# Interleaving scores with smaller v pieces, pairing head pairs in the weighted values, and beginning the first dense layer on half of its input

## The chip, the cores and the metric

One core of a Trainium2 chip runs the whole program. The metric is the device time of one execution, in microseconds. Where I speak of "the control", I mean the kernel before, run again beside each experiment on the same chip. The experiments ran on three chips, so each is held against its own control.

The engines are PE (TensorE, matmuls; PEld is its weight loads), DVE (VectorE), ACT (ScalarE) and POOL (GpSimd). PSUM is where the matmuls of this kernel put their results. The profile names tiles: tq is q transposed, ks the sorted k, tv the sorted v in PSUM and vs its copy ("eviction"), sc the scores and at their exponentials, pv the weighted values, rec their reciprocals and x the product, tr the transposed x and xt its copy, hps the first layer in PSUM, rt its rectifier output, wp the result of a filler.

## The reference, cut to what matters

```python
# P: sort_net after 5 rounds of exp and of row and column normalisation
k_sorted = einsum('bhij,bhjcd->bhicd', P, k_blocks)     # same for v
scores   = q_b @ k_sorted.T / 8
attn     = softmax(scores)                              # within blocks of 96
x        = (attn @ v_sorted), heads side by side        # 3072 x 512
h        = x @ w_in                                     # 512 -> 2048
out      = (s * relu(h)**2 + b) @ w_out                 # 2048 -> 512
```

There are 4 batches of 8 heads, 768 rows and 64 columns a head, in 8 blocks of 96 rows. The kernel works on half batches of 384 rows. Two heads make a head pair; four head pairs make the 512 inputs of the first layer. The whole argument is about the first half batch, that is, about how soon after its start PE can be given the dense layers.

## The kernel before

The pieces that matter, with cuts marked. `psa` is a pool of three PSUM buffers of 1024 floats a partition (the large pool), `psb` of two buffers of 512 (the small pool). "v" and "s" name the engine that copies a result out of PSUM, DVE or ACT. `n0` and `nn` choose blocks: the first layer takes two of the half batch's four blocks at a time.

```python
def warm_up(n, pool=psb):                  # filler: keeps PE occupied, result unused
    wp = pool.tile([128, 256], FP, ...)
    for _ in range(n):
        nc.tensor.matmul(out=wp, lhsT=zt[:, 0:128], rhs=zt, start=True, stop=True)

def v_piece0(d0, n, eng):                  # sort v of batch 0, n of its 64 columns
    ps = psa.tile(...) if n > 8 else psb.tile(...)
    for t in range(n):                     # 64 rows in use
        nc.tensor.matmul(out=ps[:, t, :], lhsT=vb[0:64, :, d0 + t], rhs=pd1[0:64]..., ...)
    evac(VS[0][:, :, d0:d0 + n], ps..., eng)

def s_piece(t, hp): ...                    # 8 score matmuls into psa, one exp on ACT -> AT[t, hp]
def p_piece(t, hp, n0, nn): ...            # weighted values of one head pair; DVE: reciprocal, product -> X
def t_part(t, hp0, eng, n0, nn): ...       # transpose two head pairs of X into XT

def ffn1(t, slot, n0, nn):                 # first layer
    for f0 in range(0, NF, 2):
        hps = psa.tile(...)                # 2 x 4 matmuls over the four head pairs
        ... relu on ACT, square on DVE ...
        slot()                             # one piece of other work

warm_up(76); build_pd1(); q_half(0, "s")
k_piece(0, 0, 16, 1, "v")(); ... k_piece(0, 80, 8, 1, "s")()
v_piece0(0, 16, "v"); v_piece0(16, 16, "s"); v_piece0(32, 16, "v"); s_piece(0, 0)
v_piece0(48, 8, "v"); s_piece(0, 1)
v_piece0(56, 8, "v"); s_piece(0, 2); s_piece(0, 3)
for hp in range(NHP):
    p_piece(0, hp, 0, 2)
    if hp == 3: t_part(0, 0, "s", 0, 2)
    warm_up(2, psa)
t_part(0, 2, "v", 0, 2)
warm_up(2, psa)
ffn1(0, Queue([P(0,0,2,2), P(0,1,2,2), P(0,2,2,2), P(0,3,2,2), ...], 8), 0, 2)
```

The softmax here doesn't subtract the row's maximum and nothing guards it: scores larger than these inputs give would overflow.

## Time and profile before

| what | value |
|---|---|
| time, first runs | 233.06 us (233.01 to 233.14, 3 runs) |
| span of the profiled run | 231.6 us, PE busy 97% |
| clock of TensorE, by the trace's clock records, which begin at 3.87 us | half from 14.11 to 27.77 us, full otherwise |
| fillers at the start | one each 0.213 us up to 3.9 us, each 0.109 us after |
| first weighted value (pv) | 23.71 us |
| first matmul of the first layer (hps) | 27.32 us by the timeline, 27.52 in the chain |

PE is the bound nearly everywhere. The chain of waits gives, for each piece of the path that ended last, its start, its length and what it was. The timeline gives each engine's instructions and, in brackets, how long the engine had been idle before and what ended that. The lines that carry the reading stand in the prediction below.

A "window" below is a stretch of 3.413 us. That is read off the clock records: in the trace of before the clock rose at 3.87 us, fell at 14.11, rose at 27.77 and fell, past the end, at 232.57, which is 10.24, 13.65 and 204.80 us apart, or 3, 4 and 60 times 3.413.

### The profile page before, as it was taken

What the parts mean: (1) busy time and instruction counts of PE and PEld (TensorE: products, weight loads), DVE (VectorE), ACT (ScalarE), POOL (GpSimd) and SP (SyncE); (2) the same over time, 40 slices, a digit from 0 to 9 for tenths busy, and PEclk for the clock granted to TensorE, in tenths of its full rate; (3) what the DMA queues carried; (4) which work ended last, traced back from release to release, by engine and by line L of the source; (5) the groups of instructions that cost most, each with busy time, mean ns of one, the idle gap of its engine ahead of it and who ended that gap; (6) DMA issues with size and microseconds to landing.
All of it is one profiled execution on the core that took longest, in us unless ns stands there. A gap on an engine that the chain in (4) does not pass through costs nothing.

```text
span 231.6 us, 4837 instructions
## 1 busy us (share of the span) xinstructions
PE 224.3 (97%) x2036; PEld 136.8 (59%) x2036; DVE 116.8 (50%) x245; ACT 114.6 (49%) x164; POOL 48.3 (21%) x62
## 2 busy tenths in 40 slices
PE   8879999999999999999999999999999999999994
PEld 6779887765544555566555555665555556554442
DVE  5778566638992645244446653343452634432221
ACT  6168479685158486856630645656222236660000
POOL 7820000399992000007920000000000000000000
PEclk9975699999999999999999999999999999999999
DMA  5999999998799992764999995610115240001212
GB/s 93 142 200 211 226 193 205 231 220 183 106 110 180 273 312 63 161 82 65 130 148 133 183 197 115 93 47 0 46 47 113 93 110 4 3 0 45 80 59 91
DMA packets 46695, 28.90 MB, mean 125 GB/s; under 512 B 35921, under 2 KB 41041, under 8 KB 46161
## 3 DMA queue, kind: packets, MB, share of 16 engines
q0 software_dynamic: 18800, 15.21, 47.8%
q1 hardware_dynamic: 27728, 13.32, 26.6%
q8 instruction: 16, 0.26, 0.5%
q10 hardware_dynamic: 144, 0.07, 0.1%
q14 instruction: 7, 0.05, 0.1%
HBM read 29.63 MB, written 8.65 MB: 165 GB/s over the span
## 4 chain that ended last, share of the span: by engine, by line
PE 82%; DVE 7%; DMA 5%; ACT 3%; issue 1%; POOL 0%; POOLq 0%
PE hps L473 35%; PE ops L516 31%; DMA qr<-in_q_dram 5%; PE pv L402 4%; PE sc L375 3%; DVE gt L478 2%; ACT ks L240 2%; DVE ks L238 2%; PE tv L320 2%; PE ops L501 2%; PE tk L294 1%; PE tv L350 1%; PE wp L182 1%; PE tq L254 1%; PE tv L336 1%
## 5 line engine op out<-in xcount | busy, mean ns | idle before, releaser
L473 PE MATMUL hps<-xt,wi 128*128 128x384 bf16 (+1 forms) x576 | 87.1, 309 | 0.3 <-ACT rt L477 0.3
L516 PE MATMUL ops<-wo,gt 128*128 128x512 bf16 x368 | 86.9, 380 | 0.4 <-DVE ot L490 0.4
L473 PEld LDWEIGHTS <-wi 128*128 128x128 bf16 x576 | 54.1, 98 | 30.6 <-issue 1.3
L477 ACT ACTIVATE rt<-hps 128x768 bf16<-128x768 f32 (+1 forms) x72 | 53.1, 741 | 37.4 <-PE hps L473 37.0
L478 DVE TENSOR_TENSOR gt<-rt 128x768 bf16<-128x768 bf16 (+1 forms) x72 | 41.2, 574 | 50.2 <-ACT rt L477 50.0
L516 PEld LDWEIGHTS <-gt 128*128 128x128 bf16 x368 | 33.6, 98 | 37.2 <-issue 1.0
L378 ACT ACTIVATE at<-sc 96x768 bf16<-96x768 f32 x32 | 24.4, 804 | 27.7 <-PE sc L375 27.7
L490 DVE SCALAR_TENSOR_TENSOR ot<-ops,s_bc,bias 128x512 f32<-128x512 f32 x23 | 17.1, 749 | 41.2 <-PE ops L516 41.2
L240 ACT CAST ks<-tk 64x512 bf16<-64x512 f32 (+1 forms) x32 | 18.6, 582 | 10.5 <-PE tk L294 10.2
L407 DVE TENSOR_TENSOR x<-pv,rec 96x512 bf16<-96x512 f32 (+1 forms) x36 | 22.6, 627 | 1.3
L639 POOL TENSOR_TENSOR csum<-csum,wo 128x512 f32<-128x512 f32 x14 | 17.6, 1254 | 1.0
L402 PEld LDWEIGHTS <-at 96*128 96x128 bf16 (+1 forms) x256 | 12.0, 104 | 3.8
L182 PE MATMUL wp<-zt 128*128 128x256 bf16 x86 | 12.9, 311 | 1.1 <-DVE warm L113 1.1
L238 DVE CAST ks<-tk 64x512 bf16<-64x512 f32 (+1 forms) x20 | 13.0, 651 | 1.1 <-PE tk L294 0.8
L402 PE MATMUL pv<-vs,at 96*128 96x66 bf16 (+1 forms) x256 | 13.0, 199 | 0.1
L240 ACT CAST vn<-tv 128x512 bf16<-128x512 f32 (+1 forms) x12 | 9.4, 799 | 7.2 <-PE tv L350 5.0
L375 PEld LDWEIGHTS <-ks 64*96 64x96 bf16 x256 | 8.6, 128 | 5.8 <-issue 5.1
L406 DVE RECIPROCAL rec<-pv 96x8 f32<-96x8 f32 (+1 forms) x36 | 6.9, 192 | 9.5 <-PE pv L402 9.4
L84 POOL DMA_DIRECT2D qr<-in_q_dram x12 | 10.6, 912 | 4.8 <-DMA kb<-in_k_dram 3.1
L375 PE MATMUL sc<-qt,ks 64*96 64x96 bf16 x256 | 10.9, 219 | 0.1
L182 PEld LDWEIGHTS <-zt 128*128 128x128 bf16 x86 | 9.0, 110 | 2.6 <-DVE warm L113 1.1
L294 PEld LDWEIGHTS <-kb 64*128 64x128 bf16 x192 | 6.7, 99 | 3.9 <-issue 3.4
(73 smaller groups left out, 98.4 us busy)
## 6 DMA issues: line engine op xcount, KB each, us to landing
out_dram<-ot SPq DMA_DIRECT2D x23, 256.0 KB, 2.4
kb<-in_k_dram POOLq DMA_DIRECT2D x4, 768.0 KB, 12.2
vb<-in_v_dram POOLq DMA_DIRECT2D x4, 768.0 KB, 19.0
wi<-in_moe_w_in_dram POOLq DMA_DIRECT2D x2, 1024.0 KB, 19.7
wo<-in_moe_w_out_dram POOLq DMA_DIRECT2D x2, 1024.0 KB, 32.6
qr<-in_q_dram POOLq DMA_DIRECT2D x12, 128.0 KB, 13.5
dv<-vn SPq DMA_DIRECT2D x6, 256.0 KB, 7.5
vs<-dv POOLq DMA_DIRECT2D x4, 384.0 KB, 12.7
```

Source lines behind the costliest of these rows:

```text
L182: nc.tensor.matmul(out=wp, lhsT=zt[:, 0:128], rhs=zt, start=True, stop=True)
L238: nc.vector.tensor_copy(out=out, in_=in_)
L240: nc.scalar.copy(out=out, in_=in_)
L375: nc.tensor.matmul(out=sc[:, e, n * BLK:(n + 1) * BLK], lhsT=ks[pr, g0 + n, :], rhs=QT[b][pr, hp, q0:q0 + BLK], start=True, stop=True)
L378: nc.scalar.activation(out=at, in_=sc[:, :, 0:TG], func=AF.Exp, scale=scale)
L402: nc.tensor.matmul(out=pv[e][0:m, (n - n0) * VW:(n - n0 + 1) * VW], lhsT=atf[:, c0:c0 + m], rhs=VS[b][:, gi, :], start=True, stop=True)
L407: nc.vector.tensor_tensor(out=x[:, n0:n0 + nn, hp * 128:(hp + 1) * 128].rearrange("p n (e d) -> p e n d", e=2), in0=pvv[:, :, :, 0:D], in1 ...
L473: nc.tensor.matmul(out=hps[:, f, 0:nt], lhsT=wi_at(hp, f0 + f), rhs=xt_at(t, hp, n0, nn), start=(hp == 0), stop=(hp == NHP - 1))
L477: nc.scalar.activation(out=rt[:, :, 0:nt], in_=hps[:, :, 0:nt], func=AF.Relu)
L478: nc.vector.tensor_tensor(out=gt[:, f0:f0 + 2, c0:c0 + nt], in0=rt[:, :, 0:nt], in1=rt[:, :, 0:nt], op=ALU.mult)
L516: nc.tensor.matmul(out=ops, lhsT=gt[:, f, m * 128:(m + 1) * 128], rhs=wo_at(f), start=(f == 0), stop=(f == NF - 1))
L639: nc.gpsimd.tensor_tensor(out=csum, in0=csum, in1=wo_at(f), op=ALU.add)
```

## The change

The intent is to have scores and exponentials ready earlier, to save DVE instructions and fillers between scores and first layer, and to fill the time of the last copy of x with matmuls that don't need it. The core of the diff, with cuts marked:

```diff
+    def p_pair(t, hp0, n0):            # weighted values of two head pairs in one psa tile
+        p2 = psa.tile([128, 4, 256], FP, tag="a", name="pv")
+        ... 16 -> 8 matmuls a pair, ONE reciprocal (96x8) and ONE product (96x512) ...
-    def ffn1(t, slot=nothing, n0=0, nn=HB):
+    def ffn1(t, slot=nothing, n0=0, nn=HB, lead=0):
+        for f0 in range(0, lead, 2):   # first two head pairs only
+            begun[f0] = psa.tile([128, 2, 512], FP, tag="a", name="hps")
+            products(f0, begun[f0], range(0, NHP // 2))
 ...
-    v_piece0(32, 16, "v")
-    s_piece(0, 0)
-    v_piece0(48, 8, "v")
-    s_piece(0, 1)
-    v_piece0(56, 8, "v")
-    s_piece(0, 2)
-    s_piece(0, 3)
     for hp in range(NHP):
-        p_piece(0, hp, 0, 2)
-        if hp == 3:
-            t_part(0, 0, "s", 0, 2)
-        warm_up(2, psa)
+        v_piece0(32 + 8 * hp, 8, "v")
+        s_piece(0, hp)
+    warm_up(2)
+    p_pair(0, 0, 0)
+    warm_up(2)
+    p_pair(0, 2, 0)
+    t_part(0, 0, "s", 0, 2)
+    warm_up(3)
     t_part(0, 2, "v", 0, 2)
-    warm_up(2, psa)
 ...
-    ffn1(0, Queue([...], 8), 0, 2)
+    ffn1(0, Queue([...], 8), 0, 2, 4)
```

## The prediction

Notes on the hardware that came from outside this case are cut from the prediction, with the cuts marked. Its sum: the first weighted value at 24.2, 3.0 of work on PE and 0.05 more give the first layer at 27.25 us; 16 of its matmuls then end at 28.98 in place of 29.17, a gain of 0.19 us, so 233.06 - 0.19 = 232.87 us. In "three runs within 0.13 us speak against that", "that" is the thought that the clock rises at another time in each execution. The 4096 slots of rival A can be had from the trace: sixteen fillers of 256 columns, 0.213 us each, fill a window. That the clock looks at such slots was my guess; part 5 holds it against the traces.

> **What bounds the kernel now.** I read the page's engine table first, then the clock row of its forty slices, then the chain of waits, then the timeline and the table by stages of the one stretch that the change touches. The engine table:
>
> ```profile
> PE 224.3 (97%) x2036; PEld 136.8 (59%) x2036; DVE 116.8 (50%) x245; ACT 114.6 (49%) x164; POOL 48.3 (21%) x62
> ...
> PEclk9975699999999999999999999999999999999999
> ```
>
> PE is busy for 97% of 231.6 us and the others for half, so whatever shortens the end must let PE start its dense layer earlier or run at a better clock. The second line shows where: slices 3 to 5 have a clock well below full. Only the start, up to about 28 us, has anything to give. After it the chain stays mainly on PE, with short runs on DVE and ACT beside a PE that is busy, so I take the last 200 us as rigid: what the start gains or loses comes out at the end.
>
> The chain of waits through the stretch (start, length, what):
>
> ```profile
> 17.16 0.75 ACT ks L240
> 17.95 2.97 PE tv L320 x32
> 20.92 0.40 PE sc L375 x8
> ...
> 22.97 0.70 DVE vs L238
> 23.71 0.38 PE pv L402 x4
> 24.09 0.43 PE wp L182 x2
> ...
> 27.10 0.43 PE wp L182 x2
> 27.52 0.84 PE hps L473 x8
> ```
>
> The reader is to see four things. PE runs v pieces and scores without a break from 17.95 to about 23.6. The first weighted value (pv, 23.71) waits for the last eviction of v on DVE, not for an exponential. From 23.71 to 27.52 PE does little real work: 16 pv, 8 transposes and ten filler matmuls (wp) of about 0.21 us each. The first layer (hps) starts at 27.52.
>
> The table by stages (stretch, length, busy us of PE, PEld, DVE, ACT, POOL, then the granted clock), cut at the times at which the clock changes:
>
> ```profile
> 17.53:20.94 3.41, 3.27 (x41) 3.22 (x41) 2.60 (x4) 3.08 (x6) 0.00 (x0) 0.50 1.13 211
> 20.94:24.36 3.42, 3.32 (x55) 3.14 (x54) 2.70 (x5) 2.64 (x4) 0.53 (x1) 0.50 1.12 212
> 24.36:27.77 3.41, 3.41 (x32) 2.77 (x31) 2.55 (x8) 0.96 (x2) 0.00 (x0) 0.50 1.17 229
> 27.77:31.18 3.41, 3.41 (x52) 3.21 (x51) 2.15 (x9) 1.76 (x4) 0.00 (x0) 1.00 1.02 196
> ```
>
> The clock is half from 14.11 to 27.77 us: 13.66 us, four stretches of 3.41. PE was "busy" for 96% of the stretch from 17.53 and 97% of the next, and the clock stayed at half; it rose only after the stretch from 24.36, which held eight of the 256-column fillers.
>
> [...] three runs within 0.13 us speak against that here, and I assume the same window edges afterwards. [...] the loads for pv start at 23.54, their matmuls at 23.71. [...] the product on 96x256 takes 420 ns, on 96x512 690 ns; 256 more elements cost 270 ns, so about 150 ns are fixed (worked out from these two).
>
> **The change, part by part.**
>
> *Scores between four v pieces of 8.* The same 64 tv and 32 sc matmuls. Before: pieces of 16, 16, 16, 8, 8; after: 16, 16 and four of 8, each followed by one score group. A pair of 8 tv and 8 sc took 20.92 to 21.88, 0.96 us. The second v piece still starts at 17.95 (ACT frees its buffer). 16 tv at 0.093 us (2.97 over 32) end at 19.44. The third piece now has 8 columns and so goes to the small PSUM pool, where by the compiled order it waits for the last cast of ks on ACT; the ACT timeline ends those at 19.66. So PE now stalls 19.44 to 19.70, +0.26, where it used to run on. Four pairs at 0.97 then end at 23.58, no earlier than before (23.6), as the work is the same. Scores and exponentials do start earlier (first exponential at about 21.0 against 21.36), but they were not what ended a wait. The last v piece now is ready at about 23.35 rather than 22.9; its eviction (0.69) ends near 24.1 to 24.2. First pv: about 24.2 against 23.71, **+0.5 us**. Two fillers moved in front of it fall into this wait and cost nothing.
>
> *Pairs of head pairs.* 4 reciprocals of 178 ns and 4 products of 420 ns (2.39 us) become 2 of 200 and 2 of 690 (the 96x8 and 96x512 forms later in this trace; 1.78 us): 0.6 us of DVE off, but the latency from pv to x grows from about 0.7 to 1.0 us. On PE: 16 pv in all about 1.3 us in two groups, 8 transposes 0.64, and after the first pv five fillers (2 + 3) rather than ten: 5 x 0.213 = 1.07. Sum 1.3 + 0.64 + 1.07 = 3.0, against 27.52 - 23.71 = 3.81. **-0.8 us.** Waits: pair 1 ends near 24.85, its x 1.0 later at 25.85; PE has two fillers (0.43) and pair 2 (0.65) in between and gets there at 25.9. Pair 2's x is ready near 26.95; PE has 4 transposes (0.32) and 3 fillers (0.64) and arrives at 26.9. So the fillers match the waits, with nothing to spare. First layer: 24.2 + 3.0 + 0.05 = 27.25, **0.27 earlier**.
>
> *First layer on two of four head pairs.* 8 of its matmuls need only the first half of xt, which ACT has copied by then (0.48 after the first transposes). They cover the DVE copy of the second half (0.36), where a filler pair stood. This is what lets fillers go; no matmul is added or removed. Two of three large PSUM buffers are held, which the compiled order shows to add no wait on an eviction still to come.
>
> *Sum.* 16 matmuls of the first layer: before they end at 29.17. After: from 27.25 at half clock (0.16 us each) three fit before 27.77, 13 at full clock take 1.07 (0.66 per 8), and one pv group lies between (0.14): 28.98. **Gain 0.19 us**, hence 233.06 - 0.19 = 232.87.
>
> **The rivals.**
>
> *A: the clock comes up one window later.* The stretch from 24.36 to 27.77 held 8 fillers, 11 pv, 8 transposes and about 2 hps; after, by my times, 5 fillers, 14 pv, 8 transposes and 3 hps. Counting moving columns weighted by the rows used, which is my estimate of what the clock looks at: before 2048 + 545 + 576 + 300 = 3470 of 4096 slots (85%), after 1280 + 690 + 576 + 580 = 3130 (76%). The initial window that released the clock held 2.74 us of fillers, 80%; the stretch from 20.94 that did not release it comes to about 68% in the same measure. So after lies between a fail and a pass. If it fails, half clock lasts to 31.18. In that window the old kernel does 4.2 groups of 8 hps at 0.81 us; at half clock about 2.2 fit: loss 2 x 0.81 = 1.6 us, giving 234.5. For it: fewer fillers, 96% busy failing before. Against it: dense hps work, and the counts 2, 2, 3 look tuned. I give it 0.3.
>
> *B: the clock comes up one window earlier*, at 24.36. The idle 0.2 us before the first pv would be filled, but the window has 24 rather than 32 sc and no more fillers. It would save about 1 us (DVE still needs its 1.0 after pair 2): 232.0. Chance 0.05.
>
> *C: the PSUM wait at 19.44 and the later last eviction cost more than the fillers give.* If PE stood idle for x twice by 0.3 us, 233.3. The timeline's 0.69 us evictions make it possible; chance 0.1.
>
> *D: all of it is hidden*: within 0.1 us of 233.06. The chain says otherwise, since pv, wp and hps follow one another on PE with no gap.
>
> **Range and chances.** The main course gives 232.87, rival A 234.5, B 232.0, C 233.3. Weighted to the middle I say 232.9, with 232.2 to 234.7 holding the outcomes. Two per cent is 4.7 us; no rival makes a third of that: 0.01 faster, 0.98 same, 0.01 slower.
>
> **What would show it.** In the changed profile: the third v piece starts near 19.70 after a wait for ACT; first exponential near 21.0; last v eviction ends at 24.1 to 24.2; first pv at 24.2; first hps near 27.25; clock change at 27.77 (31.18 if A, 24.36 if B). DVE count falls by 4 and wp matmuls by 3 (86 to 83). From 29 us on, every instruction should stand a constant 0.2 us earlier; if the shift changes later on, the rigid tail was wrong. I am wrong if the window edges move, or if PE waits longer than 0.1 us for either x.

## The result, and the profile after

The changed kernel took 234.24 us (233.82 to 234.49, 4 runs) against 233.10 (4 runs of before). The ratio is 1.0047, 95% interval 1.003 to 1.0065. Ratios here are the mean time of one kernel's runs over that of the other's in the same rounds, so not quite the ratio of the medians. So it is slower by about 1 us: within 2%, but in the direction opposite to my 0.2 us gain.

First the clock row of the profile (tenths of full speed in forty slices), after the change:

```profile
PEclk9985599999999999999999999999999999999998
```

Then the stages of the changed kernel, cut at the times of its own clock changes (columns as in the prediction: busy us of PE, PEld, DVE, ACT, POOL, then the granted clock; the last two, of DMA, are not used here):

```profile
19.65:23.06 3.41, 3.41 (x55) 3.41 (x54) 2.36 (x4) 2.77 (x4) 0.00 (x0) 0.50 1.12 211
23.06:26.48 3.42, 3.27 (x39) 2.46 (x39) 2.31 (x6) 1.45 (x3) 0.53 (x1) 0.50 1.19 229
26.48:29.89 3.41, 3.41 (x27) 3.07 (x26) 0.64 (x3) 0.96 (x2) 0.00 (x0) 0.50 1.07 219
29.89:33.30 3.41, 3.41 (x85) 3.05 (x84) 3.27 (x13) 1.97 (x4) 0.00 (x0) 1.00 1.08 182
```

The half clock ends at 29.89 us, 2.1 later than in the trace of before. The chain of waits of the changed kernel, in the same stretch that the prediction shows of before:

```profile
19.63 0.66 PE tv L320 x6
...
23.86 0.54 PE wp L182 x2
24.40 0.53 PE pv L424 x8
24.93 0.02 issue
24.95 0.21 DVE rec L429
25.17 0.02 issue
25.19 0.70 DVE x L430
25.89 0.05 issue
25.93 0.50 PE tr L467 x4
26.43 0.64 PE wp L182 x3
27.07 0.32 PE tr L467 x4
27.39 1.92 PE hps L498 x12
```

The chain is as I drew it: fillers, first pair, its reciprocal and product on DVE, transposes, fillers, first layer at 27.39 (27.52 before, in the same view). But twelve first-layer matmuls now take 1.92 us, 0.16 each, where eight took 0.84 before and then 0.66. They run at half clock (0.50 in the stretch from 26.48), and each takes 1.9 times the 0.083 us of the later eight. From 29.9 us to the end every instruction stands 0.95 to 0.97 us later than before, to within 0.03, so nothing was won or lost afterwards in this run. The 0.95 fit the clock alone: 29.89 - 27.77 = 2.12 us more at half clock, with matmuls at about half the pace, are worth about 1.06 at most by estimate, and 0.95 at the 0.45 us that part 6 finds for each microsecond.

That left two explanations. Either the change moved the clock's rise, or the two profiled executions had merely met the clock's windows at different times. I took the second as theory 1 at first, with a rise that is fixed by the kernel as its rival. Both turned out to be half right.

### The profile page after: what moved, and what is told of

The parts are those of the page before. It is cut to its first block, busy times and chain, and to the rows that moved or that the text cites. A ratio compares the mean times of both kernels' runs of the same rounds, so it can differ in the third digit from the quotient of the medians.

```text
span 232.5 us, 4807 instructions
## 1 busy us (share of the span) xinstructions
PE 224.2 (96%) x2013; PEld 137.2 (59%) x2033; DVE 116.5 (50%) x242; ACT 114.7 (49%) x164; POOL 48.6 (21%) x62
## 4 chain that ended last, share of the span: by engine, by line
PE 86%; DVE 7%; ACT 4%; issue 1%
PE hps L498 35%; PE ops L552 31%; PE wp L182 5%; PE sc L375 4%; PE pv L402 3%; ACT ks L240 3%; DVE gt L514 2%; DVE ks L238 2%; PE ops L537 2%; PE tk L294 1%; PE tv L320 1%; PE tv L350 1%; PE tq L254 1%; PE tv L336 1%; DVE qt L238 1%
## 5 line engine op out<-in xcount | busy, mean ns | idle before, releaser
L498 PE MATMUL hps<-xt,wi 128*128 128x384 bf16 (+1 forms) x576 | 88.1, 311 | 0.3 <-ACT rt L513 0.3
L552 PE MATMUL ops<-wo,gt 128*128 128x512 bf16 x349 | 83.8, 379 | 1.6 <-DVE ot L526 0.4
L498 PEld LDWEIGHTS <-wi 128*128 128x128 bf16 x576 | 54.8, 99 | 30.5 <-issue 1.3
L378 ACT ACTIVATE at<-sc 96x768 bf16<-96x768 f32 x32 | 24.5, 804 | 27.6 <-PE sc L375 27.6
L407 DVE TENSOR_TENSOR x<-pv,rec 96x512 bf16<-96x512 f32 (+1 forms) x32 | 20.9, 654 | 1.2
L402 PEld LDWEIGHTS <-at 96*128 96x128 bf16 x240 | 10.8, 103 | 3.2
L375 PE MATMUL sc<-qt,ks 64*96 64x96 bf16 x256 | 11.6, 219 | 0.1
L402 PE MATMUL pv<-vs,at 96*128 96x66 bf16 x240 | 11.5, 196 | 0.0
L406 DVE RECIPROCAL rec<-pv 96x8 f32<-96x8 f32 (+1 forms) x32 | 6.2, 194 | 9.0 <-PE pv L402 9.0
L294 PEld LDWEIGHTS <-kb 64*128 64x128 bf16 x192 | 6.1, 95 | 3.9 <-issue 3.4
```

What stands on the lines that cost most here:

```text
L375: nc.tensor.matmul(out=sc[:, e, n * BLK:(n + 1) * BLK], lhsT=ks[pr, g0 + n, :], rhs=QT[b][pr, hp, q0:q0 + BLK], start=True, stop=True)
L378: nc.scalar.activation(out=at, in_=sc[:, :, 0:TG], func=AF.Exp, scale=scale)
L402: nc.tensor.matmul(out=pv[e][0:m, (n - n0) * VW:(n - n0 + 1) * VW], lhsT=atf[:, c0:c0 + m], rhs=VS[b][:, gi, :], start=True, stop=True)
L407: nc.vector.tensor_tensor(out=x[:, n0:n0 + nn, hp * 128:(hp + 1) * 128].rearrange("p n (e d) -> p e n d", e=2), in0=pvv[:, :, :, 0:D], in1 ...
L498: nc.tensor.matmul(out=hps[:, f, 0:nt], lhsT=wi_at(hp, f0 + f), rhs=xt_at(t, hp, n0, nn), start=(hp == 0), stop=(hp == NHP - 1))
L552: nc.tensor.matmul(out=ops, lhsT=gt[:, f, m * 128:(m + 1) * 128], rhs=wo_at(f), start=(f == 0), stop=(f == NF - 1))
```

## The experiments

Means of all runs of a kernel, beside the control's mean in the same rounds:

| run | mean us | control | ratio (95%) |
|---|---|---|---|
| before again | 233.41 | 233.42 | 0.9999 (0.9983 to 1.0015) |
| after again | 234.27 | 233.42 | 1.0036 (1.0017 to 1.0056) |
| scores order alone | 234.45 | 233.42 | 1.0044 (1.0020 to 1.0069) |
| pairs and half layer alone | 233.51 | 233.42 | 1.0004 (0.9987 to 1.0021) |
| scores order, last v first | 234.06 | 233.39 | 1.0029 (1.0016 to 1.0042) |
| pairs, half layer, values one slot later | 233.85 | 233.39 | 1.0020 (1.0007 to 1.0033) |
| pairs alone | 234.36 | 233.39 | 1.0042 (1.0018 to 1.0065) |
| before with 38 more fillers | 243.44 | 233.39 | 1.0437 (1.0397 to 1.0477) |
| before, v over 128 rows | 233.98 | 233.39 | 1.0027 (1.0010 to 1.0044) |
| after, v over 128 rows | 235.15 | 233.39 | 1.0077 (1.0056 to 1.0098) |
| pairs and half layer, v over 128 rows | 234.32 | 233.39 | 1.0044 (1.0020 to 1.0068) |
| before, late fillers over 64 rows | 236.35 | 233.51 | 1.0114 (1.0097 to 1.0130) |

### 1. Both kernels again

No edit. What I expected of the kernel before:

> The kernel before, unchanged, as a control. Theory 1 (the edges of the clock's windows fall at other times from execution to execution, and the 1.1 us are where they fell): its runs should spread over some 233.0 to 234.5 once there are more of them, and its trace should show the half clock ending at a time other than 27.77 us. Theory 2 (the edges are fixed by the kernel's own work on PE): all runs at 233.0 to 233.2 and the clock up at 27.77 again.

and of the changed one:

> The changed kernel, unchanged, as a control. Theory 1: runs between 232.8 and 234.5, the early ones with the clock up near 27.8, and no difference from the control of before beyond 0.3 us in the mean. Theory 2: all at 233.8 to 234.5 again, clock up at 29.9.

Before spread over 232.93 to 233.89 in its control runs of this round (11), not over the 0.13 us of its first three. After spread over 233.65 to 234.84. The new traces show the clock up at 27.55 (before) and 28.46 (after). So the edges of the clock's windows do move from execution to execution, as theory 1 said. But the difference of 0.85 us in the mean stayed, which theory 1 denied: it allowed 0.3. The change itself costs time.

The new trace of before shows the stretches ahead of its rise so:

```profile
20.74:24.15 3.41, 3.30 (x57) 3.24 (x57) 2.50 (x3) 2.40 (x4) 0.53 (x1) 0.50 1.14 216
24.15:27.56 3.41, 3.41 (x34) 2.70 (x33) 2.51 (x9) 1.47 (x3) 0.00 (x0) 0.50 1.17 226
```

The half clock here lasted three windows (17.32 to 27.56) and not four, and yet it ended at nearly the same moment. So in these two traces it is not the number of windows that is the same but the work in the last of them: the clock rose after the window that began at 24.36 or 24.15, and not after the one that began at 20.94 or 20.74.

### 2. The change in its two halves

Scores order alone (only the loop over `v_piece0` and `s_piece` of the diff):

> Only the order of v pieces and scores is changed; weighted values, ten fillers and first layer as before. By my working the first weighted value comes at 24.3 in place of 23.7, so with the same clock edges 233.6 (+0.5). If the clock's edges decide (theory 1) its runs spread by over 0.5 us. If this part alone moves the clock (theory 2), 234.2 with the clock up later than 27.8.

Pairs and half layer alone (everything else of the diff):

> Only the pairs of head pairs, seven fillers and the first layer begun on two head pairs; v pieces and scores as before. By my working it starts the first layer 0.5 to 0.7 us earlier, so with the same clock edges 232.6. Theory 2 with the fewer fillers as the cause: the clock is up later and the time is 234 or more.

The scores order alone costs 1.0 us, as much as the whole change within the interval. (The run that was traced is the slowest of its six, 235.79 us, so its clock's rise, 30.49 us, is not the usual one.) The other half is level (+0.1), not the -0.5 to -0.8 that I expected. Its trace has the first layer at 26.99 us, and its clock up at 28.07: more than 1 us of first layer ran at half clock.

Why does the scores order cost? Its first pv came at 24.44, 0.65 later than before when the 0.08 by which PE's first transposes started later are taken off. The timeline of the changed kernel shows the first part of it, at its third v piece:

```profile
17.88 1.55 PE L320 MATMUL tv<-pd,vb 64*128 64x64 bf16 x16 [0.18 <-ACT ks L240]
...
19.63 0.66 PE L320 MATMUL tv<-pd,vb 64*128 64x64 bf16 x6 [0.21 <-ACT ks L240]
```

The third piece has 8 columns now, so it sits in the small pool and waits for ACT's last cast of ks. From second to third piece it takes 1.76 us in the scores-order trace and 1.41 before: 0.35 us lost.

### 3. The last v piece ahead again

```diff
-    for hp in range(NHP):
-        v_piece0(32 + 8 * hp, 8, "v")
-        s_piece(0, hp)
+    v_piece0(32, 8, "v"); s_piece(0, 0)
+    v_piece0(40, 8, "v"); s_piece(0, 1)
+    v_piece0(48, 8, "v"); v_piece0(56, 8, "v")
+    s_piece(0, 2); s_piece(0, 3)
```

> The kernel with the scores order alone, but the last v piece put ahead of the third score group again. Theory 1 (the scores order costs because the eviction of the last v piece, which the first weighted value waits for, ends later): the first weighted value comes 0.3 to 0.4 us earlier than the 24.4 of the scores order alone, and the mean time falls from 234.4 to about 234.0. Rival (the 0.2 us stall of the third v piece on ACT's last cast of ks is the whole cost): no change, 234.4.

Mean 234.06, and the first pv at 24.00, 0.32 earlier than with the scores order (starts corrected). Both are as expected; the intervals of the two means overlap, so the firm part is the pv. So the 0.65 us is two things: 0.35 in the wait for the small pool (still there here: 1.75 us) and 0.3 in the later eviction of the last v piece. That exponentials started earlier (20.88 against 21.36 us, in the changed kernel) brought no earlier pv, as the prediction said.

### 4. The half layer: is its gain given back?

The changed kernel's second trace has a wait that before has not. PE's timeline after the change:

```profile
29.25 0.30 PE L402 MATMUL pv<-vs,at 96*128 96x66 bf16 x4
29.39 0.83 PE L498 MATMUL hps<-xt,wi 128*128 128x192 bf16 x8
30.46 0.31 PE L402 MATMUL pv<-vs,at 96*128 96x66 bf16 x4 [0.25 <-DVE x L407]
```

and before:

```profile
29.00 0.30 PE L402 MATMUL pv<-vs,at 96*128 96x66 bf16 x4
29.14 0.83 PE L473 MATMUL hps<-xt,wi 128*128 128x192 bf16 x8
29.88 0.31 PE L402 MATMUL pv<-vs,at 96*128 96x66 bf16 x4
```

The first two rounds of the layer hold only four matmuls each now, so PE reaches the third weighted-value piece before DVE has freed its buffer. The wait is 0.25 us; the first trace of after, at half clock until 29.89 us, shows none. I tried to remove it by beginning those pieces one slot later:

```diff
-    Queue([P(0,0,2,2), P(0,1,2,2), P(0,2,2,2), P(0,3,2,2), q_half, t_piece, SC(1,0), SC(1,1)], 8)
+    Queue([nothing, P(0,0,2,2), P(0,1,2,2), P(0,2,2,2), P(0,3,2,2), q_half, t_piece, seq(SC(1,0), SC(1,1))], 8)
```

> Pairs and first layer on two head pairs, scores order as before, and the second half's weighted values begun one slot later. Theory 1 (the early start of the first layer is given back because the third weighted-value piece then waits for DVE, 0.25 us in the trace of that kernel and of the changed one): that wait is gone and the time falls by 0.25, to about 233.2. Rival (DVE sets the pace of these pieces anyway and the wait moves to a later piece or to the transposes): 233.5 as without.

The wait is gone, but a larger one stands further on:

```profile
34.70 0.67 PE L375 MATMUL sc<-qt,ks 64*96 64x96 bf16 x16
35.85 0.83 PE L498 MATMUL hps<-xt,wi 128*128 128x192 bf16 x8 [0.49 <-DVE xt L238]
```

The second half's transposes moved back with the pieces, and the next part of the layer waits for DVE's copy of them. The mean rose by 0.3 us over the kernel without this edit, with intervals that overlap. The rival was right: the wait moved.

And the half layer taken away, with pairs and seven fillers kept:

```diff
-    ..., SC(1, 0), SC(1, 1)], 8), 0, 2, 4)
+    ..., SC(1, 0), SC(1, 1)], 8), 0, 2)
```

> Pairs with seven fillers, scores order as before, first layer not begun on two head pairs. If the early start hides the DVE copy of xt (about 0.4 us in which PE now idles), the first layer's first rectifier output comes no later but the weighted-value wait of 0.25 us is gone: 233.4 to 233.6, level with the kernel that has it. If the early start was worth its full 0.4 us, 233.9.

It took 234.36, neither of my figures, and spread over 233.18 to 235.31. The trace, of the second slowest of the six runs (235.08), says why:

```profile
24.73:28.14 3.41, 3.13 (x30) 2.34 (x28) 2.08 (x5) 0.96 (x2) 0.00 (x0) 0.50 1.23 244
28.14:31.55 3.41, 3.41 (x29) 3.16 (x28) 1.32 (x5) 0.98 (x2) 0.00 (x0) 0.50 0.93 180
```

The window from 24.73 did not release the clock, and the half clock lasted to 31.55. With seven fillers and the idle wait for the copy back, PE was busy for 3.13 of its 3.41 us, and by the count of part 5 it held 74%. This speaks for a clock that depends on the kernel's work, which is rival A of the prediction.

### 5. What does a window count?

In the prediction I guessed that the clock looks at moving columns (those of `rhs`, 256 for a filler) weighted by the rows in use. At half clock a filler of 256 columns took 0.213 us, so a window of 3.413 us holds 16 of them, or 4096 columns. I added up, from the matmul records of the traces (transposes among them), columns times rows over 128 for every window at half clock, as a share of 4096, each matmul in the window in which it starts (the first window of before is at half clock by the pace of its fillers, as no clock record covers it):

| trace | did not release | released |
|---|---|---|
| before | 63% (from 20.94) | 91% (from 24.36) |
| after | 52% (19.65), 74% (23.06) | 93% (26.48) |
| scores order | 71% (23.67) | 96% (27.08) |
| pairs and half layer | 68% (21.25) | 82% (24.66) |
| values one slot later | 66% (20.61) | 74% (24.02) |
| pairs alone | 66% (21.31), 74% (24.73) | 99% (28.14) |
| before, its first window | | 81% (0.46) |

In all fourteen traces no window up to 77% released the clock, and every one from 81% did, with one exception at 74%. One filler is 6% of a window, so the edges matter: if each matmul is shared out over its duration, the exception has 79%, and the two kinds part between 75% and 78%. Columns without the rows do not separate them: 119% did not release the clock (values one slot later, from 20.61; over 100%, as matmuls over 64 rows ran in part beside each other: eight of v and eight of scores, 1280 columns, took 0.96 us in the trace of before, where five fillers of as many columns took 1.07) and 81% did (before, from 0.46). The profile's "busy" does not either: 96% and 97% busy did not release it in the kernel before. This is a rule read off the traces; what the hardware counts is not shown. The clock's fall is not counted here: in the trace of before it fell at 14.11 us, after a window in which PE was busy for 2.25 of 3.41 us, and in that of after at 16.24, after one with 2.20 of 3.42.

If this is the rule, one can slide a window over a trace and ask from which end on it holds 78%: 25.4 and 26.1 us in the two traces of before (25.4 and 25.8 counted from PE's first transposes), 26.2 with pairs and half layer alone, 27.2 and 27.3 in the traces of after, and 27.3 with the scores order. Shared out over the durations it is 25.9, 26.2, 27.2, 27.7, 27.6 and 27.5, so the figure for pairs and half layer is good to 1 us only. The release would then fall between that time and one window (3.4 us) later, by chance. These are estimates from the rule, not measured times.

Two kinds of test were spoilt, and a third was in part.

**More fillers in the kernel before** (8 ahead of the first v piece, 20 between single v matmuls, 10 elsewhere: 38 in all, by the trace too, not the 36 that I wrote down):

```diff
+        fillers(ahead)
         for t in range(n):
+            if t < n // 2: fillers(...)        # 256 columns into the unused half of ps
             nc.tensor.matmul(out=ps[:, t, :], lhsT=vb[0:64, :, d0 + t], ...)
```

> The kernel before, with 36 more filler matmuls in PE's idle times between 13 and 26 us, so that the clock's windows there stay busy. Theory 1 (the half clock between 14 and 28 us is what the start pays for): the clock stays at full past 17 us, the first layer starts near 26 us at full clock, and the time is 231 to 232 with a spread under 0.5. Rival (the stretch is bound by the casts of ACT and DVE, and the clock falls in spite of the fillers): 234 to 237, as fillers at half clock stand in the way.

The clock held to 22.45 us, but a filler and a v matmul in turn took 0.42 us a pair at full clock, where fillers in a row take 0.11 each and v matmuls in a row 0.09, no less than at half clock (32 of them in 2.97 us in the trace of before). So in this trace the pieces of v gain little from a full clock. The first pv came at 31.95, and the time was 243.4. The rival's range was passed, for a reason that neither had: matmuls over 64 and over 128 rows in turn were dear here (0.42 us a pair against 0.11 + 0.09). The run says nothing on the rule.

**v over 128 rows**, of which 64 are zero, so that the same v matmuls weigh double:

```diff
-            nc.tensor.matmul(out=ps[:, t, :], lhsT=vb[0:64, :, d0 + t], rhs=pd1[0:64]...)
+            nc.tensor.matmul(out=ps[:, t, :], lhsT=vb[:, :, d0 + t], rhs=pd1...)
```

In the kernel before:

> The kernel before, with its v pieces multiplied over 128 rows, of which 64 are zero (same matmuls, same columns, same results; ACT writes the zeros in its idle time before 13 us). Theory 1 (a clock window counts moving columns times rows in use, and needs about 78% of its slots): counted on the traces, the first window that can release the clock ends near 24.1 us in place of 25.4, so the clock comes up 1.3 us earlier on average and the mean falls from 233.4 to 232.7 to 233.0. Rival (the clock looks at whether PE is occupied, or only at fillers): 233.4, unchanged.

in the changed kernel:

> The changed kernel with the same 128-row v pieces. Theory 1 (most of the changed kernel's loss is a later release of the clock): counted on its traces, the first window that can release the clock ends near 24.0 in place of 27.2, so the mean falls by about 1 us, from 234.25 to 233.0 to 233.4, and its distance to the kernel before with the same rows shrinks from 0.85 to 0.3 to 0.5. Rival (the loss is in the order of the work): still 0.85 above e_rows.

and in pairs and half layer:

> Pairs and first layer on two head pairs, scores order as before, with the 128-row v pieces. Theory 1: the first window that can release the clock ends near 23.7 in place of 26.2, 1.2 us of full clock won in a stretch in which PE works without a break: 232.4 to 232.8, below the kernel before. Rival (its fewer fillers or its wait for DVE set the time): 233.4 as before.

All three missed: +0.6, +0.9 and +0.8 us over the same kernel with 64 rows, in place of a gain. The timeline of PE in the first of them:

```profile
21.44 0.93 PE L324 MATMUL tv<-pd,vb 128*128 128x64 bf16 x8
22.30 0.55 PE L379 MATMUL sc<-qt,ks 64*96 64x96 bf16 x8
22.78 0.93 PE L324 MATMUL tv<-pd,vb 128*128 128x64 bf16 x8
```

With 64 rows, v matmuls and scores had run in part beside each other: a group of eight of each took 0.96 us. Now it takes 1.34 (21.44 to 22.78). The first pv moved back by 0.8 us in the kernel before and by 1.1 in the changed one (starts corrected), and the windows held no more than earlier (69% from 21.48 and 60% from 22.25: not released, as the rule says). The edit changed the pace along with the count, so it could not test the rule by its time.

**Late fillers over 64 rows** turns it round: the count falls, the number of matmuls, their columns and their order stay.

```diff
-            nc.tensor.matmul(out=wp, lhsT=zt[:, 0:128], rhs=zt, start=True, stop=True)
+            nc.tensor.matmul(out=wp, lhsT=zt[0:rows, 0:128], rhs=zt[0:rows], start=True, stop=True)
-        warm_up(2, psa)
+        warm_up(2, psa, 64)                    # and the one after the loop
```

> The kernel before with its ten late fillers multiplied over 64 rows in place of 128: the same number of matmuls, the same 256 columns, the same order and waits. Theory 1 (a clock window counts moving columns times rows in use, and needs about 78% of its slots): counted on the traces, the first window that can release the clock ends near 29.0 us in place of 25.4, so the trace shows it coming up between 29.0 and 32.5, and with 0.41 us lost per us of half clock in the first layer the mean rises by 1.0 to 1.4, to 234.4 to 234.8. Rival (the clock looks at whether PE is occupied, whatever the rows): clock up by 27.5 to 28.9 as in the control, 233.4.

```profile
23.98:27.39 3.41, 3.41 (x27) 1.69 (x27) 2.16 (x8) 1.18 (x3) 0.02 (x1) 0.50 1.20 232
27.39:30.80 3.41, 3.41 (x24) 2.41 (x23) 0.65 (x3) 0.89 (x2) 0.00 (x0) 0.50 0.97 192
30.80:34.22 3.42, 3.42 (x28) 3.18 (x27) 2.11 (x8) 0.98 (x2) 0.00 (x0) 0.50 1.21 201
```

PE is busy for all of every window by the profile. The window from 23.98 counts 47% and did not release the clock, where the same work with 128-row fillers released it from 24.15 in the control. The next counts 77% and did not either; the third, 94%, did. The time rose by 2.8 us, twice what I expected (the 0.41 us for each us of half clock was an estimate; the first four traces of part 6 give 0.99 us over 2.49, or 0.40), and the release at 34.22 lies outside my 29.0 to 32.5. The first layer also began 1.2 us later after the first pv (4.76 us against 3.58 in the control): four values and two fillers took 0.87 us in place of 0.65, the extra time standing where values of 96 rows and fillers of 64 meet (0.18 us from the last value to the first filler in place of 0.05, 0.35 from the second filler to the next value in place of 0.21). So the pace changed here too. The direction and the windows are those of the rule. A clock that looks only at whether PE is occupied does not fit the window from 23.98, as far as the profile's busy time tells. This run alone does not part columns from columns times rows, since the window also held fewer columns (77% against 102% in the control's); the counts above do.

### 6. What a microsecond of half clock costs

The start of the fourth rectifier output, counted from the first matmul of the first layer, against the half clock that was left at that matmul:

| trace | half clock left, us | to the fourth output, us |
|---|---|---|
| before again | none (-0.05) | 3.45 |
| before | 0.45 | 3.57 |
| scores order, last v first | 1.39 | 4.02 |
| scores order | 2.44 | 4.44 |
| pairs alone | 4.31 | 5.48 |

From the first to the last that is 2.03 us over 4.36, about 0.45 us for each microsecond (late fillers over 64 rows, with 5.51 us left, took 5.88, which fits). With the half layer the curve starts higher: 4.21 at 1.08 and 4.32 at 1.31, some 0.3 above the others (this holds the wait of part 4), and 4.65 at 2.70, where it meets them.

## Why the prediction was right or wrong

The time fell within my range and within the 2% that I gave 0.98, but the predicted gain of 0.19 us was a loss of 0.85 to 1.1. So the range was luck in part: it reached 234.7 only because rival A stood in it, at 234.5.

**What held.** The order of PE's work was right nearly everywhere: third v piece predicted at 19.70 after a wait for ACT, measured 19.63; first exponential 21.0, measured 20.88; last v eviction ended 24.1 to 24.2, measured 24.23; first pv 24.2, measured 24.29; first layer 27.25, measured 27.19. The fillers nearly matched the waits: PE stood idle for 0.15 us before the first transposes, until DVE had written x, a little over the 0.1 that I had allowed. And the tail was rigid in this run.

**The step that failed** is this one: "three runs within 0.13 us speak against that here, and I assume the same window edges afterwards". Three runs were too few: the edges do not keep their time from execution to execution. The clock rose at 27.55 and 27.77 us in two traces of one kernel, at 28.46 and 29.89 in two of the other, where I had named 27.77, 31.18 or 24.36. I had also written "I am wrong if the window edges move", and they did. By the counts of part 5, the clock rose after the first window that held 81% or more, but for one trace in which 74% did. I had worked out the sum with a rise at 27.77 for both kernels. In its place I estimate, by the rule of part 5, an earliest release at about 25.6 us before and 27.3 after (starts corrected), each followed by up to 3.4 us of chance.

Rival A had what the counts support, a release that depends on the work in a window, and even the measure (74% for a window that failed against 81% for one that passed, where I had guessed "between a fail and a pass"), though its counts were rough: 85% and 68% for two windows of before in which the trace gives 91% and 63%. Its size was wrong. I took it as one whole window more or none, 1.6 us with a chance of 0.3. By the rule of part 5 it is, as an estimate, a shift of about 1.7 us of the earliest release, in every execution.

An estimate of the whole from these numbers: if every phase is equally likely, the clock of after is up at 27.3 to 30.7, on average 1.75 us after the first layer began at 27.25, which costs 1.75 x 0.45 = 0.79 us. For before, 25.6 to 29.0: it is up after the first layer's start at 27.3 in half of the cases, then by 0.85 on average, 0.19 us. The difference is 0.6. The wait of the half layer adds up to 0.25. That makes 0.6 to 0.85 of the 0.85 measured (the interval of the control is 0.4 to 1.3). It is an estimate; no run held the phase fixed, and a loss near 118 us (below) stands outside it.

**A term that was mis-sized.** "First layer: 0.27 earlier" compared 27.25 with the 27.52 of the chain. In the same view the chain shows 27.39 after, so the gain was 0.13, and counted from PE's first transposes (which start 0.08 earlier in this run) only 0.05. By an estimate from part 6 (0.45 us lost for each microsecond of half clock) an earlier first layer is worth only about half while the clock is low: this would be why pairs and half layer alone, which begin it 0.4 us earlier (14.42 us after the first transposes against 14.83), came out level; no run separates it from the wait of part 4.

**Missed.** "Two of three large PSUM buffers are held, which ... add no wait": the wait came in the small pool, on DVE, two slots later. And DVE's count fell by 3 (245 to 242), not 4: the last four pieces of v take four evictions on DVE, where it had three.

**Left open.** In four of the fourteen traces (changed kernel, scores order, pairs and half layer, values one slot later) PE lost a further 0.2 to 0.85 us near 118 us, where weighted values wait for v read back from memory (0.5 us in the second trace of after). Neither trace of before shows it, nor does the first trace of after. In the second trace of after it is large: ACT's work stands 0.59 us later than in the first trace of before up to 115 us, and 1.29 from 118 us on. So it can be as large as the loss at the start; whether the edits make it more likely is not shown. Nothing that I ran was faster than the kernel before.

## What to carry to other kernels

Before judging a change of a fraction of a per cent that touches a stretch at half clock, run both kernels often enough to see the spread (0.96 us over eleven runs of before, where the first three had shown 0.13), and read the time of the clock's rise from each trace: with no change at all it differed by 0.2 us between two traces of before and by 1.4 between two of after. In this kernel, what raised the clock was told best by columns times rows inside one window: up to 77% did not, from 81% did, with one exception at 74%. Busy time did not tell it: windows with PE busy for 96% to 100% did not raise the clock, and one with 80% (2.74 of 3.41 us, the first of before) did. Moving the dense part back by 0.65 us cost 1.0 us here. A smaller piece can land in another buffer pool and inherit another wait (0.35 us here), and an exponential that is ready earlier (20.88 against 21.36 us) was worth nothing where an eviction ended the wait.
